# Attention plus MLP layer, one core: where the weight loads are issued, the first projections per token half, and a new written-out order

## The chip, the cores and the metric

The kernel runs on one core of one Trainium2 chip. The metric is device time in microseconds (us). The kernel before takes 318.64 us as the median of five runs (317.17 to 320.43). Its profiled execution took 318.41 us, of which 316.7 us lie between its first and its last instruction (its span).

## The reference, cut to what matters

Sequence 2048, model width 640, 32 heads of 20 columns, MLP width 1728, bf16 in and out.

```
xn = layernorm(x);  q, k, v = xn @ wq, xn @ wk, xn @ wv
for s in range(4):                      # segments of 512 tokens
    p = softmax(q_s k_s^T * scale + causal mask);  a_dot = p v_s
    a_mem = phi(q_s) M / (phi(q_s) z + 1e-6)
    o_s = sigmoid(beta) * a_mem + (1 - sigmoid(beta)) * a_dot
    M += phi(k_s)^T v_s;  z += sum(phi(k_s))      # phi(t) = t+1 if t>0 else exp(t)
h = x + o @ wo
out = h + silu(layernorm(h) @ w1) @ w2
```

## The kernel before, in words

The 2048 tokens are 16 blocks of 128, and four blocks make a segment. For each segment the kernel declares a list of small tasks, each of them a few instructions on one engine. The names below are those of the tasks.

- **Norm.** `n1_st` (statistics, VectorE, L705), `n1_rs` (GpSimd, L714 and L716), `n1_ap` (apply, VectorE, L722), and then a transpose into `xT`. For segment 0 the transpose is a matmul with the identity (`n1_tp`, L731) that ScalarE or VectorE empties (`n1_te`, L740/741); later it is a DMA transpose (`n1_tr`, L746). `n2_*` is the second norm, into `hT`.
- **Weights.** wq and wk arrive raw and are copied into head-padded form in five parts each (`re_wq0` to `re_wk4`, L686/688).
- **Projections.** `pr<s><c><w>` is chunk c of q (w=0) or k (w=1) for the 512 tokens of segment s: five matmuls of 512 columns (L801), emptied by `qe` on ScalarE or VectorE (L811/812). `v<s><i>` is v for one block (L773). `vt<s><n>`, twelve small copies from SBUF to SBUF, collect what is left of the heads into `QKV` (L838); score groups 5 to 7 read it.
- **Attention.** `qk` (scores, L874), `e` (exp on ScalarE, L885), `mk` (causal mask on GpSimd, L897), `av` (L920), `oe`, `tn`, `nm` (VectorE), for eight groups of four heads; segment 0 has them per token half, `x` and `y`. Groups are numbered through: 8s+g.
- **Memory.** `ex` and `ph` build phi, `kt` transposes phi(k) by DMA (L1033), `mz`, `ma` and `mb` update M and z.
- **Back.** `ot` transposes the attention output by DMA (L1094), then `wo` (L1102), the residual `rs` (L1110), the second norm, `h1` (L1126), tanh `th` (ScalarE, L1134), `s` (VectorE, L1140), `h2` (L1157), `o` (L1167), and the store `out` (L1171).

The order of all tasks, and which PSUM bank and which of two engines each uses, is written out by hand in the string `ORDER`; every engine runs its own tasks in the order in which they stand there. A tracker puts in the semaphore waits. `fill54` and its like are matmuls on zeros that keep TensorE running.

All DMAs are issued on SyncE, in one queue. The bulk loads (wo, five parts of w1, five of w2, blocks 8 to 11 of x) carry an `after`: they also wait until a certain attention step of segment 0 has written its output:

```
tick0 = lambda g, h: (f"nm{g}{h}", lambda: [(segs[0]["ot"], [(2 * (h == "y"), g)])])
load_w("wo", ..., after=tick0(0, "x"))
```

Of the kernel before, what the change touches and what calls it, by code (L numbers as in the profile page):

```python
# [5 lines left out]
ACT = mybir.ActivationFunctionType  # L6
# [228 lines left out]
class Graph:  # L235
# [51 lines left out]
    def schedule(self):  # L287
# [3 lines left out]
        for row in ORDER:  # L291
# [14 lines left out]
            t.eng = {"A": AC, "D": DV, "G": PO}[eng] if eng else list(t.engs)[0]  # L306
# [18 lines left out]
D = 640  # L325
# [20 lines left out]
QUAD_SEGS = (0, 1, 2, 3)  # L346

# [8 lines left out]
zpad:0 iota sel epsc x0:0 vpad0 mt2 x2:1 n1_st0:0 x1:2 x3:3 w_q:0 n1_st2:2 mta2 halfc mt0 mt1 n1_rs0 n1_st1:1  # L356
n1_st3:3 epsg0 n1_ap0:0 n1_rs2 fill54:0 n1_tp0:0 n1_te0/A:0 n1_rs1 n1_rs3 n1_ap1:1 n1_ap2:2 n1_tp1:2 n1_te1/A
n1_ap3:0 re_wq0/D:0 n1_tp2:4 n1_te2/D n1_tp3:6 n1_te3/A beta pr000:4 w_k zf0 re_wq1/A pr010:6 lsc0 re_wk0/D:0
re_wk2/A pr001:5 re_wk1/D lsc1 mta1 lsc2 re_wk3/A qe000/D:0 pr011:7 w_wv:0 x4:4,5,6,7 qe001/A qe011/A:0 ex011:0 lsc3
re_wq4/D re_wq2/D pr020:5 qk0x0:0 e0x2:0 e0x0 qe010/D pr031:7 pr021:6 qk1x0:0 vpad1 mtb1 mm5 mm1 mk0x n1_st5:3  # L360
qe020/D:0 ph011:0 qe021/D n1_rs5 v00:4 n1_st6:1 n1_ap5:0 re_wk4/D qe031/A:0 re_wq3/A ex001:1 n1_st4:3 n1_st7:2
e1x2:1 e1x0 v01:6 mk1x pr030:0 ve00/A:0 ex021:0 ve01/A qk2x0:4 qe030/A av1x:1 ex031:2 av0x:2 e2x2:0 pr041:3 pr040:0
oe1x/A:0 e2x0 mt3 n1_rs4 qk3x0:4 e3x0:1 e3x2 n1_rs7 mta3 mtb3 mm11 mk2x n1_rs6 vt06:0 oe0x/D:1 ph001:1 vt09 kt01:0
vt03 tn0x:1 qe041/D:0 kt00:1 ex041:1 v03:2 qe040/D ph031:0 qk0yb0:4 nm0x:0,0 v02:0 e0yb2:0 ve03/D ph021:1 e0yb0
qk0ya0:4 tn1x:2 ve02/D nm1x:0 e0ya2:0 e0ya0 mk0yb mk3x av2x:3 oe2x/D:0 qk4x0:0 av0y:4 e4x2:0 e4x0 n1_ap6:2 av3x:6
mz00:5 tn2x:7 oe0y/D:1 oe3x/D:0 zf1 n1_ap7:1 nm2x:0 qk1yb0:0 vt00 vt010 vt08 vt01 ma00/A:0 e1yb2:0 e1yb0 n1_ap4:3
vt05 n1_tr5:0 mk4x v11:4 ve11/A:1 mk1yb mtb2 mm10 vt07 n1_tr6 vt04 vt011 vt02 mz01:7 qk1ya0:0 tn0y:6 nm0y:0 ma01/D:1
v12:4 ve12/D av4x:7 e1ya2:0 e1ya0 n1_tr4 n1_tr7 oe4x/A:1 tn3x:6 qk5x0:0 e5x0:0 e5x2 mm3 mk5x tn4x:7 nm3x:0 v10:4
qk6x0:0 kt03:0 nm4x:1 e6x0:1 kt02:1 v13:6 e6x2 ve10/D av5x:4 oe5x/D:1 ve13/A qk7x0:0 pr100:5 qe100/D:0 ph041:1
e7x0:0 mz02:4 e7x2 ma02/A:2 mk6x av6x:6 qk2yb0:0 mta0 mk7x e2yb2:1 e2yb0 mk2yb mtb0 tn5x:5 pr101:4 w_w2_1:0 w_w1_0:0  # L370
w_wo:0 oe6x/D:1 av7x:6 nm5x:1 av1y:7 w_w1_3 oe7x/D:0 qk2ya0:0 ex100:1 tn6x:6 qe101/D e2ya2:0 e2ya0 nm6x:1 ex101:0
pr130:5 tn7x:6 pr110:4 nm7x:1 qk3ya0:0 pr111:6 qe110/A:0 ph100:0 ph101:0 pr121:4 oe1y/D:0 ot0:0 qe111/D e3ya2:1
e3ya0 qk3yb0:0 e3yb0:0 wo0:6 qe130/D:0 e3yb2 qe121/D:0 ex110:0 rs0 w_w1_1 ot1 mm0 mzc0 av2y:4 oe2y/A:1 n2_st0:3
qk4ya0:0 mm9 mzc1 mk3yb mm6 mzc6 n2_rs0 mm2 wo1:6 rs1 n2_st1:1 w_w2_0 w_w1_4 n2_ap0:1 e4ya2:0 e4ya0 mz03:4 w_w1_2
qk4yb0:0 kt10:1 e4yb2:1 e4yb0 av3y:5 tn2y:6 pr141:7 n2_rs1 n2_tr0:0 mzc2 mzc3 mb00:0 mk4yb ma03/D:3 nm2y:1 n2_ap1:3
n2_tr1 ex111:1 qk5ya0:0 pr140:4 oe3y/A:1 qe141/A:0 tn3y:7 e5ya0:1 nm3y:1 e5ya2 pr120:6 mz10:7 tn1y:5 qk5yb0:0
qe120/A qe140/D av4y:4 ma10 nm1y:1 oe4y/D:0 ph110:0 e5yb2:0 h1_0_8_0:5 e5yb0 h1_0_1_0:7 th0_8_0:0 ex140:2 th0_1_0:1
tn4y:4 qk6ya0:0 pr131:6 e6ya2:0 e6ya0 s0_1_0:0 nm4y:1 s0_8_0 ph111:0 h1_0_0_0:7 th0_0_0:0 w_w2_2 s0_0_0 qe131/D
mk5yb h1_0_13_0:4 th0_13_0:1 qk6yb0:0 h1_0_10_0:5 h1_0_11_0:7 av5y:6 s0_13_0 e6yb0:1 e6yb2 w_w2_4 x8:8,9,10,11
# [850 lines left out]
```

## Time and profile before

| what | value |
|---|---|
| median of five runs | 318.64 us |
| the profiled execution's own time | 318.41 us |
| its span | 316.7 us |
| TensorE (PE) busy / VectorE (DVE) / ScalarE (ACT) / GpSimd (POOL) | 302.1 / 219.9 / 227.1 / 145.2 us |
| chain that ended last, by engine | PE 73%, ACT 10%, DVE 9%, DMA 3% |
| mean granted TensorE clock | 0.994 |
| weight load wq / wk / wv, issue to landing | 7.1 / 8.7 / 10.4 us |

Busy time of PE is modelled to the end of each matmul, so short groups overlap their own start-up. "Busy" is then no proof that columns stream without gaps. The chain goes back from the last instruction, at each step to what released it. SPq is SyncE's queue of DMA issues, and the idle time in brackets behind an instruction is that of its engine just before it, with what ended it.

### The profile page before, as it was taken

How to read it: one execution, taken by the hardware profiler on the slowest of the kernel's cores; microseconds unless marked ns; L12 is line 12 of the kernel's file. 1: busy time of each engine (PE TensorE's matmuls, PEld its weight loads, DVE VectorE, ACT ScalarE, POOL GpSimd, SP SyncE). 2: the span in 40 equal slices, each digit the busy share in tenths (PEclk: the TensorE clock that was granted, in tenths of full speed). 3: DMA queues.
4: the chain of work that ended last, by engine and by line, in shares of the span. 5: the costliest groups of instructions: out<-in, count | busy, mean ns of one | idle time of the engine just before them, and what ended most of it. 6: DMA issues, size and time to landing. Idle time of an engine off the chain costs nothing.

```text
span 316.7 us, 7256 instructions
## 1 busy us (share of the span) xinstructions
PE 302.1 (95%) x2894; PEld 167.6 (53%) x2894; DVE 219.9 (69%) x488; ACT 227.1 (72%) x322; POOL 145.2 (46%) x282
## 2 busy tenths in 40 slices
PE   8899899999989999999979999999999999999996
PEld 6544444566544555655434544545554457654563
DVE  7778667778878766859987776569866676824703
ACT  1698998899988999889879896778769941004500
POOL 5446652623667565566845345444852831300000
PEclk9999999999999999999979999999999999999999
DMA  6813478967164300032672200041460005330002
GB/s 190 287 23 65 87 213 211 251 175 91 33 122 94 64 2 3 9 70 64 133 117 41 60 2 0 2 92 25 67 83 2 0 2 124 64 106 20 0 2 104
DMA packets 48353, 24.56 MB, mean 78 GB/s; under 512 B 38848, under 2 KB 47232, under 8 KB 48320
## 3 DMA queue, kind: packets, MB, share of 16 engines
q1 hardware_dynamic: 48320, 24.10, 33.9%
q8 instruction: 23, 0.38, 0.5%
q14 instruction: 10, 0.08, 0.1%
HBM read 10.33 MB, written 2.62 MB: 41 GB/s over the span
## 4 chain that ended last, share of the span: by engine, by line
PE 73%; ACT 10%; DVE 9%; DMA 3%; issue 2%; SPq 1%; POOL 1%; DVEq 0%; ACTq 0%
PE ps_all L1157 18%; PE ps_all L1126 18%; PE ps_all L801 10%; PE ps_all L1102 6%; PE ps_all L874 6%; PE ps_all L773 5%; PE ps_all L920 4%; ACT PTE L885 3%; PE ps_all L607 3%; ACT PTB L885 2%; DMA oT<-otok 2%; ACT PTA L885 2%; PE ps_all L949 2%; PE ps_all L953 1%; DMA hT<-xn_rot 1%
## 5 line engine op out<-in xcount | busy, mean ns | idle before, releaser
L1126 PE MATMUL ps_all<-hT,w_sb 128*128 128x512 bf16 (+3 forms) x350 | 69.0, 342 | 1.3 <-DMA hT<-xn_rot 0.8
L885 ACT ACTIVATE PTA<-ps_all 128x1024 bf16<-128x1024 f32 x64 | 62.5, 1028 | 8.4 <-PE ps_all L874 7.5
L1157 PE MATMUL ps_all<-w_sb,sT 128*128 128x320 bf16 x448 | 67.2, 300 | 0.4 <-DVE on L986 0.3
L885 ACT ACTIVATE PTB<-ps_all 128x1024 bf16<-128x1024 f32 (+1 forms) x64 | 59.0, 972 | 8.2 <-PE ps_all L874 8.2
L897 POOL TENSOR_SCALAR_AFFINE_SELECT PTB<-PTB 128x512 bf16<-128x512 bf16 x64 | 40.9, 638 | 43.5 <-ACT PTB L885 41.1
L1134 ACT ACTIVATE th<-ps_all 128x512 f32<-128x512 f32 (+2 forms) x70 | 34.8, 524 | 34.5 <-PE ps_all L1126 30.2
L1140 DVE SCALAR_TENSOR_TENSOR sT<-th,ps_all 128x512 bf16<-128x512 f32 (+2 forms) x70 | 38.9, 576 | 24.1 <-ACT th L1134 23.4
L1157 PEld LDWEIGHTS ps_all<-w_sb,sT 128*128 128x128 bf16 x448 | 40.7, 98 | 24.1 <-issue 7.2
L1126 PEld LDWEIGHTS ps_all<-hT,w_sb 128*128 128x128 bf16 (+1 forms) x350 | 31.8, 99 | 30.6 <-issue 7.2
L885 ACT ACTIVATE PTE<-ps_all 128x1024 bf16<-128x1024 f32 (+1 forms) x40 | 35.9, 946 | 5.1 <-PE ps_all L874 4.7
L897 POOL TENSOR_SCALAR_AFFINE_SELECT PTE<-PTE 128x512 bf16<-128x512 bf16 x40 | 25.7, 641 | 24.3 <-ACT PTE L885 22.9
L705 DVE BATCH_NORM_STATS2 stt<-x_tok 128x6 f32<-128x320 bf16 x64 | 28.0, 479 | 1.9 <-DMA x_tok<-in_A_x_dram 1.5
L1167 DVE SCALAR_TENSOR_TENSOR x_tok<-ps_all,x_tok 128x640 bf16<-128x640 f32 x16 | 13.0, 823 | 19.9 <-PE ps_all L1157 19.7
L1102 PE MATMUL ps_all<-wo_sb,oT 128*128 128x320 bf16 x160 | 24.1, 299 | 2.0 <-DMA oT<-otok 1.1
L801 PE MATMUL ps_all<-xT,wqr 128*128 128x512 bf16 x100 | 24.6, 380 | 0.9 <-ACT xT L740 0.9
L801 PE MATMUL ps_all<-xT,wkr 128*128 128x512 bf16 x100 | 24.4, 380 | 0.0
L773 PE MATMUL ps_all<-wv_sb,xT 128*128 128x320 bf16 x160 | 24.2, 299 | 0.1
L994 POOL TENSOR_TENSOR otok<-on 128x320 bf16<-128x320 bf16 x24 | 19.1, 799 | 11.3 <-DVE on L986 11.3
L812 DVE CAST QK<-ps_all 128x512 bf16<-128x512 f32 x28 | 19.0, 683 | 7.4 <-PE ps_all L801 6.7
L874 PE MATMUL ps_all<-QK 20*128 20x256 bf16 (+3 forms) x360 | 20.8, 288 | 3.0 <-DVE oTs L935 1.8
L897 POOL TENSOR_SCALAR_AFFINE_SELECT PTA<-PTA 128x512 bf16<-128x512 bf16 x24 | 15.4, 641 | 12.3 <-ACT PTA L885 12.3
L935 DVE TENSOR_SCALAR oTs<-ps_all,lsc 128x512 bf16<-128x512 f32 (+1 forms) x25 | 15.6, 628 | 7.3 <-PE ps_all L920 7.0
(78 smaller groups left out, 406.5 us busy)
## 6 DMA issues: line engine op xcount, KB each, us to landing
out_dram<-x_tok SPq DMA_DIRECT2D x16, 160.0 KB, 1.9
w_sb<-in_B_w_dram SPq DMA_DIRECT2D x5, 432.0 KB, 6.0
x_tok<-in_A_x_dram SPq DMA_DIRECT2D x3, 640.0 KB, 6.0
w_sb<-in_B_w_dram SPq DMA_DIRECT2D x3, 640.0 KB, 4.6
QKV<-QK SPq DMA_DIRECT2D x16, 72.0 KB
sT<-in_A_wq_dram SPq DMA_DIRECT2D x1, 800.0 KB, 7.1
sT<-in_A_wk_dram SPq DMA_DIRECT2D x1, 800.0 KB, 8.7
wv_sb<-in_A_wv_dram SPq DMA_DIRECT2D x1, 800.0 KB, 10.4
```

The lines of the kernel that those rows point to most:

```text
L705: T.add(DV, lambda e, hh=hh: e.bn_stats(out=stt[:, s, 6 * hh:6 * hh + 6], in_=xb[:, 320 * hh:320 * hh + 320]), reads=R((xa, xsub)), writes ...
L773: fns.append(lambda e, c=c, hh=hh: e.matmul(bank(ps, hh)[:, 0:320], lhsT=xT[:, c, 128 * i:128 * i + 128], rhs=wv_sb[:, c, 320 * hh:320 * h ...
L801: fns = [lambda e, kc=kc: e.matmul(bank(ps), lhsT=wt[:, kc, c, :], rhs=xT[:, kc, :], start=(kc == 0), stop=(kc == NC - 1)) for kc in range ...
L874: fns.append(lambda e, j=j, o=o, r=r, q0=q0, q1=q1, qa=qa, ka=ka: e.matmul(ps_all[:, o:o + q1 - q0], lhsT=ka[32 * r:32 * r + DH, 128 * j:1 ...
L885: T.add(AC, lambda e: e.activation(out=pt[:, pta.slot, q0:q0 + 2, 0:width], in_=sc3[:, b0:b0 + 2, 0:width], func=ACT.Exp, scale=SCALE), re ...
L897: fns.append(lambda e, v=v: e.affine_select(out=v, in_=v, pattern=[[0, 4], [1, 128]], compare_op=ALU.is_ge, fill=0.0, base=0, channel_mult ...
L994: T.add(PO, lambda e: e.tensor_tensor(out=o_dst, in0=on[:, ona.slot, 0, :].rearrange("p (i x) -> p i x", i=4), in1=on[:, ona.slot, 1, :].r ...
L1102: fns.append(lambda e, c=c, hh=hh: e.matmul(bank(ps, hh)[:, 0:320], lhsT=oT[:, c, 128 * i:128 * i + 128], rhs=wo_sb[:, c, 320 * hh:320 * h ...
L1126: fns = [lambda e, c=c: e.matmul(bank(ps)[0:fw, lo:hi], lhsT=w1_sb[:, c, 128 * f:128 * f + fw], rhs=hT[:, c, lo:hi], start=(c == 0), stop= ...
L1134: T.add(AC, lambda e: e.activation(out=th[0:fw, tha.slot, lo:hi], in_=bank(ps)[0:fw, lo:hi], func=ACT.Tanh, scale=0.5), reads=R((ps, [0])) ...
L1140: T.add(DV, lambda e: e.scalar_tensor_tensor(out=sT[0:fw, f, lo:hi], in0=th[0:fw, tha.slot, lo:hi], scalar=1.0, in1=bank(ps)[0:fw, lo:hi], ...
L1157: fns.append(lambda e, f=f, fw=fw, hh=hh: e.matmul(bank(ps, hh)[:, 0:320], lhsT=sT[0:fw, f, 128 * i:128 * i + 128], rhs=w2_sb[0:fw, f, 320 ...
```

## The change

It has five parts.

1. The loads of wq, wk and wv are issued on ScalarE's DMA queue, ahead of any other work there but a table load and one tiny exp (`warm`). x blocks 0 to 3 and beta stay on SyncE.
2. The bulk loads lose their `after`. In its place they read the region of `re_wk0`'s result, which means that the first of them waits for that copy; from there on only their place in SyncE's queue counts. Blocks 4 to 7 of x (`x4`), which were the ninth issue, without any wait, come under the same rule. `x8` and half of the weights stand right behind it, ahead of the first copy into `QKV`.
3. Chunks 0 and 1 of the projections of segment 0 are made per token half: five matmuls of 256 columns for blocks 0 and 1, and five for blocks 2 and 3. Score tasks of the `x` half wait only for their own half.
4. The parts of h2 are (0,4), (4,7), (7,10), (10,14), w2 is loaded in the same parts, and each part waits for its own piece of w2.
5. `ORDER` is new throughout: 1374 entries in place of 1364. 43 entries name ScalarE and 76 name VectorE, where 45 and 70 did. The zero matmuls are 40, 11, 6 and 3, all near the start; they were 54 at the start, and 2 and 4 just before the first `h1` of segment 1.

The constants with which a planner outside this file weighs tasks (`pe_c`, the `bw` values, `0.4` to `0.46` and the like) change too; no instruction depends on them.

```
-    load_w("q", wraw[:, 0, :, :], cw(A_wq), -96, 2.5, [(sT0, ["q"])])
+    G.task("warm", {AC: 0.3}, lambda e_: T.add(AC, lambda e: e.activation(
+        out=warm[:, :], in_=zpad[:, 0:1], func=ACT.Exp), reads=R((C, ["zpad"])), writes=R((C, ["warm"]))),
+        [(C, ["zpad"])], [(C, ["warm"])], -100)
+    load_w("q", wraw[:, 0, :, :], cw(A_wq), -99, 6.2, [(sT0, ["q"])], "fix", (AC,))
+    load_w("k", wraw[:, 1, :, :], cw(A_wk), -98, 7.8, [(sT0, ["k"])], "fix", (AC,))
+    load_w("wv", wv_sb[:, :, :], cw(A_wv), -97, 9.5, [(W["wv"], [0])], "fix", (AC,))
...
-    load_x(4, 4, -90)
-    load_w("wo", wo_sb[:, :, :], cw(A_wo), 0, 2.5, [(W["wo"], [0])], after=tick0(0, "x"))
...
+        dma("w_" + k, [(W["wk"], [0])] if kind == "plain" else [], wr, lambda e: e.dma_start(out=dst, in_=src), prio, bw, kind, engs=engs)
...
+                for hh, (b0, b1) in enumerate([(0, 2), (2, 4)] if s == 0 and c in SPLIT0 else [(0, 4)]):
...
+                        fns = [lambda e, kc=kc: e.matmul(bank(ps)[:, lo:hi], lhsT=wt[:, kc, c, :], rhs=xT[:, kc, lo:hi],
+                                                         start=(kc == 0), stop=(kc == NC - 1)) for kc in range(NC)]
...
-            parts = ((0, 4), (4, 8), (8, 11), (11, 14))
+            parts = ((0, 4), (4, 7), (7, 10), (10, 14))
+            W2P = ([0], [1], [2], [3, 4])
```

The start of the new order, and its stretch just before the first `h1` of segment 1:

```
zpad:0 warm w_q:0 w_k w_wv:0 mt2 epsc iota vpad1 mt1 vpad0 halfc x0:0 x1:1 x2:2 x3:3 beta sel n1_st0:0 mt0 n1_rs0
n1_st1:2 n1_ap0:0 mt3 fill40:0 n1_tp0:0 mta3 n1_rs1 n1_st3:0 n1_ap1:0 re_wq0/D:0 n1_rs3 fill11:2 n1_tp1:2 n1_ap3:1
n1_st2:2 re_wk1/D:0 n1_te0/A:0 re_wq1/A n1_te1/A fill6:4 n1_tp3:0 n1_te3/A lsc0 pr010x:2 pr000x:3 pr011x:0
...
n2_rs4 n2_st7:0 rs6 wo5:6 mz14:4 qk18a0:0 mb12:0 mb10:0 mk17a n2_ap4:0 n2_rs7 vt27 vt211 vt23 e18a2:0 out2 e18a0
vt26 n2_tr4:0 rs5 n2_ap7:1 n2_tr7 av17:5 h2_3_0:6 qk19b0:0 h2_3_1 n2_st6:2 ma14 e19b0:1 oe17/D:0 tn17:4 h2_3_2 e19b2
qk19a0:0 n2_st5:0 mk18b mk18e n2_rs6 n2_ap6:1 n2_rs5 mk18a mk19b e19a2:1 e19a0 mk19a nm17:1,1 vt25 out0 h2_3_3 vt24
vt28 n2_tr6 mz13:4 n2_ap5:0 o3 ma13 av18:5 n2_tr5 qk20b0:0 tn16:6 av19:4 oe18/D:0 ad17:0 e20b0:0 nm16:1,0 e20b2
oe19/A:1 h1_1_6_0:5 qk21b0:0 th1_6_0:1 s1_6_0:0 tn18:6 e21b2:1 e21b0 nm18:1,1 h1_1_5_0:4 h1_1_1_0:5 th1_5_0:1 out3
```

## The prediction

> **What bounds the kernel now.** I read the page's busy shares first, then a table of busy time by stage, then the chain, then the timeline where the table showed a hole.
>
> ```profile
> PE 302.1 (95%) x2894; PEld 167.6 (53%) x2894; DVE 219.9 (69%) x488; ACT 227.1 (72%) x322; POOL 145.2 (46%) x282
> ```
>
> PE looks full, but it is not streaming all the time. I count the columns of all matmuls from the order, with four row or column tiles side by side counted once, at the rate of the chain's pieces "five matmuls of 512 columns in 1.08 us" (2370 columns per us). They are 266 us, 6.5 of it matmuls on zeros. So some 50 us of 316.7 are waits and group starts. Where they lie is the question.
>
> ```profile
> 12.00:160.00 148.00, 140.78 (x1551) 78.74 (x1549) 112.56 (x276) 133.81 (x199) 84.66 (x166) 1.00 0.45 100
> 170.00:260.00 90.00, 89.38 (x874) 46.50 (x873) 63.16 (x125) 72.39 (x93) 46.14 (x74) 1.00 0.20 33
> 260.00:316.70 56.70, 53.53 (x338) 31.48 (x336) 27.70 (x48) 9.78 (x17) 4.02 (x9) 1.00 0.22 59
> ```
>
> The columns are stretch, PE, PEld, DVE, ACT and POOL busy, clock, DMA share, GB/s. From 170 on PE idles 0.6 us in 90, and then only to the end of the last store; an order gains little there. After the last score group both orders leave the same 60 us of columns. So the change is decided before 170, where ACT (90% busy to 160) and PE wait for each other. PE's real holes to 170, from the timeline: 0.9 at 11.6, 1.4 at 32 to 35, 1.1 at 47 to 57, 1.8 at 89 to 96, 2.05 at 157.5 to 162.6. The last is the largest:
>
> ```profile
> 158.94 3.55 DMA hT<-xn_rot
> 162.57 2.29 PE ps_all L1126 x5
> ```
> ```profile
> 157.50:162.60 5.10, 3.05 (x47) 1.67 (x46) 4.77 (x11) 4.60 (x7) 3.19 (x6) 0.99 1.11 211
> 162.60:167.00 4.40, 4.40 (x20) 1.40 (x21) 3.53 (x9) 2.75 (x5) 1.45 (x4) 0.62 0.26 40
> ```
>
> The chain waits for the last transposed block of the second norm, then five matmuls take 2.29 us instead of 1.08. The clock is 0.62 for 4.4 us, which costs 0.38 x 4.4 = 1.7.
>
> **The stretch before the first h1 of segment 1: 3.5 us gained.** Before, the last `wo` ends at 154.7 and `h1` starts at 162.57: 7.9 us with 3.7 us of useful columns (plus 0.65 of zeros). PE needs 3.7/0.84 = 4.4 for them (0.84: the share at which columns run in the ACT-bound stage, an estimate from 121 us of columns between 11.6 and 162.6, taken without its holes). Lost: 3.5, and 1.7 of clock, 5.2 together. After, 7.9 us of columns stand between the same two points (the last `wo` is wo5), so PE has 9.4 us of work. The chain there is longer: DVE does rs5, ap7, st6, ma14, oe17, st5, ap6, nm17, ap5, by rows 0.8+0.45+1.1+0.3+0.7+1.1+0.45+1.4+0.45 = 6.7, then the transpose 3.55, 10.3 in all. PE waits 0.9, and I give the clock drop 4 chances in 10 (0.7). Gain 5.2 - 1.6 = 3.6, say 3.5; bounds 0 and 5.2.
>
> A rule speaks on the clock. The Trainium skill, "TensorE: Matmul & The Clock Gate", section "What's actually happening", has the slow state after an idle window of about 3.4 us. Here the longest single idle time is 0.77 and the sum 2.05 in 5.1, and the clock fell all the same. By the rule a new order with waits under 3.4 us loses no clock, and the gain here is 4.3; by the row, light work of short groups is enough, and each such stretch may cost 1.7. I follow the row.
>
> **The start: 0.3 us gained (bounds 1.5 each way).** Removed: wq, wk, wv from SyncE's queue, x4's early issue (2.54 us of issuing at 4.76). Added: three issues on ACT (0.43+0.43+0.53) and `warm`; ACT idles 7.6 us there, so they cost nothing; with ACT busy they would cost their 1.4.
>
> ```profile
> 11.59 2.33 PE L801 MATMUL ps_all<-xT,wqr 128*128 128x512 bf16 x10 [0.89 <-ACT xT L740]
> 12.47 0.77 DVE L688 COPY wkr<-sT 128x400 bf16<-128x400 bf16 x4 [1.22 <-DMA sT<-in_A_wk_dram]
> ```
>
> wq lands at 9.8, wk at 12.4. After, GpSimd does a second set of pads (1.9 us) ahead of the first `n1_rs`: it ends at about 6.4 in place of 5.15. The 40 zero matmuls end at 1.12+40x0.152 = 7.2, tp0 at 7.5; eleven (1.7) and tp1 to 9.5; six and tp3 to 10.7. ACT then does re_wq1 (0.85), te1 and te3 (0.65 each), and the first projection starts at about 10.9 if wq lands by 9, 11.3 if at 9.8: 0.3 to 0.7 earlier. The k halves wait for wk plus two copies (0.9). The first exp comes near 16.5 in place of 17.49. But ACT has then done 4 us less of its work, and at score group 4 both orders have as much PE and ACT work behind them; so most of that second is not a gain.
>
> Here a rule speaks against the change: the Trainium skill, "DMA: Bandwidth & Descriptors", section "Issuing engines are not separate DMA queues": a second issuing engine saves only issue time, as all run on the same 16 DMA engines. By it wk lands near 12.2 (beta's 0.52 no longer ahead). The row of 4 to 8 us has DMA share 0.81 and of 0 to 4 0.55: were that filled, 4x0.19 = 0.8 and part of the first stretch are gained, and wk lands near 11. I take 11.5.
>
> Halves: 2x0.65 in place of 1.08 to 1.19 for four projections, 0.5 to 0.9 us of PE; eight evacuations of 256 columns, nearest row 0.48 (128x256 to oTs) against 0.60 to 0.68, 1.4 us in all on ACT and DVE. PE waits for wk in this stretch, which hides it; without that cover it costs 0.9.
>
> **The bulk loads: 0.7 us gained to 60 us (bounds 2.6 gained, 1 lost).** The DMA has room early and none later:
>
> ```profile
> 16.00:20.00 4.00, 4.00 (x33) 1.54 (x32) 2.53 (x7) 3.74 (x7) 0.86 (x2) 1.00 0.01 4
> 52.00:56.00 4.00, 3.56 (x31) 1.68 (x32) 2.44 (x5) 3.54 (x5) 0.34 (x1) 1.00 1.06 189
> ```
>
> The oT transposes at 50 to 57 share with the weights, and half of 1.1 us of holes is what a freer DMA can give back. Now the new wait: x4 waits for `re_wk0`, about 12.9, and behind it in SyncE's queue stand x8, half the weights (2752 KB to the first QKV copy), then 1232 KB among those copies: 4.08 MB. At 327 GB/s (row of 8 to 12) 12.5 us; copies and transposes took 0.41 of 20 to 40, 8.3 us. 12.9+12.5+8.3+2 to land = 35.7, and QKV was first read at 39.39. At 239 GB/s (4 to 8) it is 40.3, 1 us late. So it mostly fits. DVE's st5 waits for x4, at about 14.6 to 16, a stall in which its next evacuation isn't due until 19. h2's own w2 parts cost nothing: all of w2 was there before 77.5, and comes earlier.
>
> **89 to 96: 1.0 us gained of 1.8.** Before, `ot2` stands 0.6 us of columns ahead of `wo2` and `ot3` none ahead of `wo3`, against 2.6 to 3.6 us for the transpose (PE waits 0.69). After they stand 5.4 and 3.4 ahead.
>
> **Elsewhere: 1.5 us lost.** A wholly new order has new meetings of ACT, POOL and PE that no row shows; the holes listed are 7.3 us in 150, and I let it make a fifth of them anew. Bounds 0 and 4. Evacuations move: ACT has some 2 us less in all, DVE 3.5 more; DVE is 76% busy to 160, so nothing on the path.
>
> Sum: -3.5 -0.3 -0.7 -1.0 +1.5 = -4.0. From the profiled execution's 318.4 that is 314.4; the median, 318.64, is 0.2 higher.
>
> **Rivals.** (a) The order only moves its holes: the stretch at 157 keeps half its gain, elsewhere as much is lost: 318.4 -1.8 +1.5 = 318.1. For it: ACT is 90% busy to 160 and its work hardly shrinks. Chance 0.15. (b) All holes close, with ACT at 95%: 318.4 - 7.3 - 1.7 = 309.4. For it: those waits are short and of many kinds, so an order can meet them. Against: DVE is later than before at `ap5`. 0.13. (c) Slower, by the unpaced x loads: DVE takes its tasks in order, and st5 and st11 wait for x4 and x8. A 640 KB load of x took 2.3 to 11.5 us. If x4 lands later than 17 (4 us after issue) and x8 after 21, DVE empties no PSUM, PE stops up to 5 us and the clock falls (1.7): 314.4 +6.7 +0.5 = 321.6. It decides from a landing of 6 us on. Against: the 11.5 was behind 2.4 MB in the same queue, here only wv's rest. 0.12. The forecast has 0.60.
>
> **Numbers.** A measurement tells from no change only more than about 0.5%, 1.6 us. Faster by more: forecast, (b), together 0.73; within: (a) less its edges, 0.14; slower: (c) and a little of (a), 0.13. The range takes the forecast's bounds, (a) and most of (b): 309.2 to 319.3.
>
> **What would show it.** The stretch before the first h1 of segment 1: PE idle under 1 us and no row of clock below 0.9. First exp on PTE at 16 to 17. wk's landing 11 to 12. QKV copies landed before the first score of group 5. No DVE wait for x_tok above 2 us. PE columns from 170 on as before. Wrong if x4 or x8 hold DVE, if the clock falls in the first 20 us, or if ACT's idle time to 160 isn't smaller than 14.2.

## The result and the profile after

| | before | after |
|---|---|---|
| median | 319.02 us (45 runs) | 316.58 us (24 runs) |
| lowest to highest | 317.17 to 322.06 | 314.98 to 318.11 |
| profiled execution, own time | 318.41 us | 315.29 us |
| its span, its mean clock | 316.7 us, 0.994 | 313.6 us, 1.000 |

The ratio is 0.992, with a 95% interval of 0.9902 to 0.9939. So the change gains 2.4 us, where 4.0 was forecast; the two profiled executions differ by 3.1.

The executions of both kernels fall into two groups by their mean granted clock, and this bears on everything below. Ratios and counts here use the executions within 1.5% of the fastest of their kernel, which are 48 of the 52 of before that ran beside after and beside the experiments. Of these 48, 23 had a clock of 0.998 or more, with a median of 317.65 us, and 25 a lower one, with 319.66. Of 25 executions of after, 12 were at 0.998 or more (315.28) and 13 lower (316.94). The profile of before is one of the lower kind, that of after one of the higher.

The first line of the profile after, engine busy times and instructions:

```profile
PE 301.9 (96%) x2914; PEld 168.9 (54%) x2914; DVE 224.8 (72%) x491; ACT 225.6 (72%) x324; POOL 144.7 (46%) x282
```

Busy time of PE is 0.2 us less than before, and the span is 3.1 us less: what was won is waiting time. Busy time by stretch, after (stretch, PE, PEld, DVE, ACT, POOL, clock, DMA share, GB/s):

```profile
160.00:165.00 5.00, 5.00 (x39) 2.13 (x38) 3.08 (x7) 4.99 (x8) 1.76 (x3) 1.00 0.45 131
...
12.00:160.00 148.00, 142.49 (x1589) 80.14 (x1587) 118.64 (x283) 134.52 (x202) 82.08 (x162) 1.00 0.43 96
...
80.00:90.00 10.00, 9.80 (x104) 5.85 (x103) 6.34 (x15) 9.97 (x16) 6.16 (x11) 1.00 0.44 85
90.00:100.00 10.00, 9.94 (x98) 5.33 (x97) 8.19 (x20) 9.28 (x12) 5.39 (x11) 1.00 0.63 102
```

The same two stretches of before:

```profile
80.00:90.00 10.00, 9.30 (x97) 5.42 (x95) 8.16 (x22) 9.38 (x13) 6.30 (x14) 1.00 0.30 51
90.00:100.00 10.00, 8.83 (x94) 4.70 (x93) 7.97 (x19) 8.73 (x11) 7.35 (x14) 1.00 0.55 113
```

From 12 to 160 us PE is busy 1.7 us more, and 1.6 of that lies between 80 and 100: the hole of 89 to 96 is gone. In the row of 160 to 165 the clock is 1.00, where before has 0.75, with the 0.62 of 162.6 to 167 in it. The chain there, after (start, us, what):

```profile
155.94 3.39 DMA hT<-xn_rot
...
159.38 1.25 PE ps_all L1131 x5
```

The last transposed block of the second norm still ends the chain, and takes as long as before (3.39 us against 3.55). But PE had other work for all but 0.20 us of it, and the five matmuls of `h1` take 1.25 in place of 2.29. That stretch went as forecast. The start did not. DMA issues of the first 20 us, after (kind, issuing queue, number, KB each, median us from issue to landing):

```profile
sT<-in_A_wq_dram ACTq DMA_DIRECT2D x1, 800.0 KB, 5.3
...
x_tok<-in_A_x_dram SPq DMA_DIRECT2D x4, 160.0 KB, 5.1
```

Before, from the same view:

```profile
x_tok<-in_A_x_dram SPq DMA_DIRECT2D x4, 160.0 KB, 3.1
```

The row of 4 to 8 us, in which these loads share the DMA engines, first after, then before. The last number, what they moved, is 378 GB/s in place of 239:

```profile
4.00:8.00 4.00, 4.00 (x28) 3.10 (x27) 1.66 (x6) 0.00 (x0) 2.04 (x7) 1.00 1.06 378
```
```profile
4.00:8.00 4.00, 4.00 (x32) 3.27 (x31) 3.39 (x11) 0.00 (x0) 2.39 (x8) 1.00 0.81 239
```

And the timeline after, where these loads are waited for (start, busy us, engine, what, idle time before it and what ended it):

```profile
8.97 0.89 DVE L704 BATCH_NORM_STATS2 stt<-x_tok 128x6 f32<-128x320 bf16 x2 [2.28 <-DMA x_tok<-in_A_x_dram]
...
12.04 1.15 PE L806 MATMUL ps_all<-xT,wqr 128*128 128x256 bf16 x9
```

wq, issued at 1.1, lands at 6.4 in place of 9.75, but the small x blocks take 5.1 us in place of 3.1. VectorE waits 2.28 us for block 3, and the first projection starts at 12.04, 0.45 later than before. Two further waits stand out. The first, 1.15 us, is longer than the one that before has at that place (0.91 us, at 32.67). It lies in the stretch in which the bulk loads, the copies into `QKV` and the `xT` transposes share SyncE's queue, and behind it, at 35.16, PE waits another 0.37 for the transposed block 5. The second, at an output projection near the end, is new:

```profile
33.49 0.40 PE L878 MATMUL ps_all<-QK 20*128 20x256 bf16 x8 [1.15 <-DVE otok L972]
```
```profile
263.99 1.26 PE L1107 MATMUL ps_all<-wo_sb,oT 128*128 128x320 bf16 x8 [0.73 <-DMA oT<-otok]
```

To see where the two kernels part, I read off when each trace has the same number of matmul columns behind it. Columns are counted in us at the prediction's rate, and matmuls on zeros are left out, as the two kernels have them in different places; 259.9 us remain in either. At 5 to 15 us of columns, after is 0.7 to 1.0 us behind before; at 30 to 65 it is 2.0 to 2.9 behind, at 70 to 120 0.6 to 1.6. At 125 it is 3.6 ahead, from there on 2.9 to 4.1, and it ends 3.1 ahead. So the first 65 us lose, and the gain comes in two places: some 2.0 us at the hole of 89 to 96 (from 65 to 70 us of columns), and 4.7 in the stretch before the first `h1` of segment 1 (from 120 to 125).

### The profile page after: what moved, and what is told of

It is laid out like the page before. It is cut to its first block, busy times and chain, and to the rows that moved or that the text cites. A ratio compares the mean times of both kernels' runs of the same rounds, so it can differ in the third digit from the quotient of the medians.

```text
span 313.6 us, 7306 instructions
## 1 busy us (share of the span) xinstructions
PE 301.9 (96%) x2914; PEld 168.9 (54%) x2914; DVE 224.8 (72%) x491; ACT 225.6 (72%) x324; POOL 144.7 (46%) x282
## 4 chain that ended last, share of the span: by engine, by line
PE 70%; ACT 13%; DMA 7%; DVE 5%; issue 2%; SPq 2%; POOL 1%; ACTq 0%; DVEq 0%
PE ps_all L1163 18%; PE ps_all L1131 15%; PE ps_all L806 11%; PE ps_all L878 7%; PE ps_all L1107 6%; PE ps_all L772 5%; ACT PTA L889 4%; PE ps_all L924 4%; ACT PTB L889 4%; ACT PTE L889 3%; DMA x_tok<-in_A_x_dram 2%; DMA QKV<-QK 1%; DVE sT L1145 1%; DMA oT<-otok 1%; PE ps_all L957 1%
## 5 line engine op out<-in xcount | busy, mean ns | idle before, releaser
L1131 PE MATMUL ps_all<-hT,w_sb 128*128 128x512 bf16 (+3 forms) x350 | 67.5, 337 | 0.4 <-DMA hT<-xn_rot 0.2
L1163 PE MATMUL ps_all<-w_sb,sT 128*128 128x320 bf16 (+1 forms) x448 | 67.7, 300 | 0.0
L1139 ACT ACTIVATE th<-ps_all 128x512 f32<-128x512 f32 (+3 forms) x70 | 35.1, 519 | 35.3 <-PE ps_all L1131 30.2
L1145 DVE SCALAR_TENSOR_TENSOR sT<-th,ps_all 128x512 bf16<-128x512 f32 (+3 forms) x70 | 39.0, 574 | 26.4 <-ACT th L1139 25.8
L1163 PEld LDWEIGHTS ps_all<-w_sb,sT 128*128 128x128 bf16 (+1 forms) x448 | 40.7, 98 | 22.5 <-issue 7.9
L901 POOL TENSOR_SCALAR_AFFINE_SELECT PTE<-PTE 128x512 bf16<-128x512 bf16 x40 | 25.5, 638 | 30.3 <-ACT PTE L889 28.9
L806 PE MATMUL ps_all<-xT,wqr 128*128 128x512 bf16 (+1 forms) x110 | 24.8, 361 | 0.4 <-ACT QK L814 0.4
L806 PE MATMUL ps_all<-xT,wkr 128*128 128x512 bf16 (+1 forms) x110 | 25.0, 361 | 0.0
L815 DVE CAST QK<-ps_all 128x512 bf16<-128x512 f32 (+1 forms) x31 | 20.1, 655 | 6.0 <-PE ps_all L806 5.7
L713 POOL TENSOR_TENSOR rst<-mvt,eps_c 128x1 f32<-128x1 f32 x32 | 6.7, 209 | 30.9 <-DVE mvt L707 30.9
L990 DVE TENSOR_TENSOR on<-ps_all,rd 128x640 bf16<-128x640 f32 x24 | 19.8, 824 | 0.8
```

Of the source, the lines that this page charges most:

```text
L806: fns = [lambda e, kc=kc: e.matmul(bank(ps)[:, lo:hi], lhsT=wt[:, kc, c, :], rhs=xT[:, kc, lo:hi], start=(kc == 0), stop=(kc == NC - 1)) f ...
L815: (lambda e: e.tensor_copy(out=o, in_=i_))
L901: fns.append(lambda e, v=v: e.affine_select(out=v, in_=v, pattern=[[0, 4], [1, 128]], compare_op=ALU.is_ge, fill=0.0, base=0, channel_mult ...
L1131: fns = [lambda e, c=c: e.matmul(bank(ps)[0:fw, lo:hi], lhsT=w1_sb[:, c, 128 * f:128 * f + fw], rhs=hT[:, c, lo:hi], start=(c == 0), stop= ...
L1139: T.add(AC, lambda e: e.activation(out=th[0:fw, tha.slot, lo:hi], in_=bank(ps)[0:fw, lo:hi], func=ACT.Tanh, scale=0.5), reads=R((ps, [0])) ...
L1145: T.add(DV, lambda e: e.scalar_tensor_tensor(out=sT[0:fw, f, lo:hi], in0=th[0:fw, tha.slot, lo:hi], scalar=1.0, in1=bank(ps)[0:fw, lo:hi], ...
```

## The experiments

The theory was that of the prediction, now with its places: the new order wins in those two stretches; the second queue and the unpaced loads by themselves win nothing. The rivals were that the holes only move, that early loads or early weights are the gain, and that later stages take up what the start loses. Each run's ratio is to before on the same chip; against after, medians are compared.

**1. The stretch put back into after.** In `ORDER`:

```
-... rs6 wo5:6 mz14:4 ... rs5 n2_ap7:1 n2_tr7 av17:5 h2_3_0:6 qk19b0:0 h2_3_1 ... h2_3_2 ... h2_3_3 ... o3
+... rs6 h2_3_0:6 h2_3_1 h2_3_2 h2_3_3 o3 mz14:4 ... n2_ap7:1 n2_tr7 av17:5 wo5:6 rs5 qk19b0:0 ...
```

> The kernel after, with only the stretch before the first h1 of segment 1 put back to the arrangement of before: h2_3_0 to h2_3_3 and o3 run ahead of the last output projection (wo5), whose residual and second norm then have little behind them to cover them. Theory: PE waits 1.5 to 2.5 us for the transposed hT, the clock falls to about 0.6 for some 4 us, and 2.5 to 4.5 us of the gain go, so that it stands at 319 to 321, at or above before. Rival (the stretch is not where the gain is; PE has slack later that takes it up): under 1 us slower than after.

Measured: 322.69 us, ratio 1.0108 (1.0064 to 1.0151), 6.1 above after. The stretch by stages:

```profile
155.00:160.00 5.00, 1.74 (x23) 0.60 (x20) 4.53 (x12) 2.74 (x4) 1.34 (x4) 0.86 0.45 101
160.00:165.00 5.00, 3.95 (x44) 1.78 (x48) 3.04 (x7) 2.32 (x4) 3.39 (x6) 0.50 0.68 103
```

PE is busy 5.7 us of 10 and the clock falls to 0.50. Up to 115 us of columns the trace is within 1.1 us of after; at 125 it is 6.3 behind, and it stays 6.1 to 6.5 behind to the end. So the stretch is where the gain is. The loss is above the forecast's 2.5 to 4.5, and much of it is clock: at 0.86 and 0.50 the two rows lose 3.2 us. All six executions of this kernel had a mean clock of 0.989 or less, so here the fall came every time. That the wait itself is long because VectorE, which has nine tenths of its time filled from 155 to 160, gets its work for the last block only after the last output projection is my reading of the order; no run tests it. The same trace, whose order up to 146 us is that of after, shows something else:

```profile
32.00:34.00 2.00, 0.58 (x16) 0.12 (x8) 1.97 (x6) 2.00 (x5) 1.32 (x3) 1.00 0.78 107
...
36.00:38.00 2.00, 2.00 (x15) 0.81 (x14) 1.80 (x4) 0.47 (x1) 1.03 (x2) 0.50 0.52 98
```

After the wait of 32 to 34 us the clock is 0.94, 0.50 and 0.71 in the next three rows of two microseconds: 1.7 us of clock, as much as at 162 in the profile of before. In the profiled execution of after the same wait left the clock at 1.00.

**2. The stretch repaired in before, first try.** `wo6` is taken up ahead of the four parts of `h2_3`, which go down behind it:

```
-... wo4:2 ... h2_3_0:0 qk18b0:4 tn16:2 h2_3_1 h2_3_2 ... h2_3_3 ... wo7:2 ... wo6:0 ... av17:2
+... wo4:2 ... wo6:0 qk18b0:4 tn16:2 ... wo7:2 ... h2_3_0:0 ... av17:2 h2_3_1 ... h2_3_2 h2_3_3
```

> The kernel before, with nothing of the change but a repaired stretch before the first h1 of segment 1: the last output projection (wo6) goes up ahead of h2_3_0 to h2_3_3, and the four parts of h2_3 go down behind it as cover for its residual, second norm and transpose. Theory (most of the gain is this stretch: waits 1.8 plus the clock drop 1.7): 3 to 3.5 us faster than before, PE idle ahead of the first h1 of segment 1 under 0.6, five h1 matmuls in 1.1 to 1.3 us, no row of clock 0.62 there. Rival (the waits only move on, ACT is the bound to 170 us): within 1 us of before. Rival (the gain of the new order lies in the hole of 89 to 96 and many small ones): 1 to 1.7 us faster, the clock alone.

Measured: 329.16 us, ratio 1.0271 (1.0216 to 1.0325). Neither the theory nor a rival held, and the chain says why:

```profile
150.20 0.58 SPq L1169
...
150.84 3.88 DMA oT<-otok
...
154.76 2.85 PE ps_all L1100 x10
```

L1169 is the line of the stores, and `ot7` is issued behind one. The parts of `h2_3` had been what PE did until `ot7` landed; without them `wo7` waits, and its ten matmuls take 2.85 us instead of 1.53, at a clock of 0.50 from 155 to 160. Nor is the wait before `h1` gone: the last transposed block lands at 173.36, after 4.40 us, and `h1` starts at 173.45. Besides what is shown, the edit moves some small tasks of the same stretch (x12, o3, out3 and parts of the second norm of block 6).

**3. The stretch repaired in before, second try.** Only `wo6` and its residual, statistics, `n2_rs` and apply go up; `h2_3` stays ahead of `wo7`:

```
-... h2_3_0:0 qk18b0:4 tn16:2 h2_3_1 h2_3_2 nm16:0,1 ... wo7:2 ... rs7 n2_st7:1 ... wo6:0 ... mk18a rs6 n2_st6:3 n2_rs7 ...
+... h2_3_0:0 qk18b0:4 wo6:2 h2_3_1 h2_3_2 rs6 n2_st6:0 tn16:2 nm16:0,1 ... wo7:2 ... rs7 n2_st7:1 n2_rs7 ... mk18a ...
```

> The kernel before, with the stretch before the first h1 of segment 1 repaired in another way than by taking the parts of h2_3 out (that left wo7 waiting for its transposed oT): only wo6 goes up, five microseconds, behind h2_3_0, with its residual, statistics and apply; h2_3 stays ahead of wo7. Theory (the stretch itself is worth its waits and its clock): the first h1 of segment 1 starts 1.5 to 3.5 us earlier than 162.57, no row of clock 0.62 there, and the time is 1.5 to 3.5 us below before. Rival (VectorE is the bound there, 94% busy from 157.5 to 162.6, so moving matmuls only moves the wait): within 1 us of before.

Measured: 323.7 us, ratio 1.0149 (1.0104 to 1.0193), and `h1` starts at 169.65. The timeline:

```profile
159.26 0.19 POOL L712 TENSOR_TENSOR rst<-mvt,eps_c 128x1 f32<-128x1 f32 x1 [2.93 <-DVE mvt L706]
...
162.09 0.64 POOL L895 TENSOR_SCALAR_AFFINE_SELECT PTA<-PTA 128x512 bf16<-128x512 bf16 x1
...
162.78 0.62 PE L918 MATMUL ps_all<-PTA,Vx 128*32 128x512 bf16 x4 [2.77 <-POOL PTA L895]
```

My edit had put `n2_rs7` ahead of the causal mask `mk18a` on GpSimd. GpSimd then stood 2.93 us waiting for VectorE's statistics, the mask behind it came late, and `av18` waited 2.77 us for the mask; after that the clock was 0.66 from 160 to 170. In the profiles of both tries, moreover, the clock fell at 34 to 38 us as in experiment 1, in a part that is not edited, which is 1.3 us of either sum. (This edit also takes the apply of block 7 and the transposes of blocks 6 and 7 up.) So the two tries do not show what the stretch alone would be worth in before. They show that an order is not repaired by moving one engine's task: what came with PE's move, a task of two short instructions on GpSimd, made the wait.

**4. wq, wk, wv back on SyncE.**

```
-    load_w("q", ..., "fix", (AC,))      # and k, wv
+    load_w("q", ..., "fix", (SP,))      # ORDER: x3:3 w_q:0 w_k w_wv:0 beta
```

> The kernel after, with wq, wk and wv issued on SyncE behind the four single x blocks, as before; ScalarE keeps only its table load and the tiny exp. Theory (the second queue brings wq early but slows the x blocks, so it gains nothing): x3 lands at about 6 in place of 8.97, wq near 10, first projection at 11.3 to 12.1, time within 0.6 us of after either way. Rival (the second queue is worth its 0.3 to 1 us): 0.5 to 1.5 us slower than after. Rival (the second queue costs): 0.5 to 1 us faster.

Measured: 315.29 us, ratio 0.988 (0.9844 to 0.9916), 1.3 below after. The first projection starts at 10.97 instead of 12.04. But then:

```profile
13.90 0.23 ACT L614 ACTIVATE bsel<-beta_bc 128x32 f32<-128x32 bf16 x1 [2.06 <-DMA beta_bc<-in_A_beta_dram]
...
14.85 0.34 PE L876 MATMUL ps_all<-QK 20*128 20x256 bf16 x8 [1.38 <-ACT QK L812]
```

beta, now last in the queue, lands at 13.88, ScalarE waits for it in `lsc0`, and the copies for the first scores stand behind. So most of the 1.07 was lost again at once, and the trace ends 0.5 ahead of after. The other 0.8 of the medians may lie in the clock: 5 of 6 executions were at 0.998 or more, against 12 of 25 of after. At such clocks alone the medians are 314.88 and after's 315.28, and the intervals overlap, so it is not shown that this version is faster than after.

**5. The second queue alone, in before.**

```
-    load_w("q", wraw[:, 0, :, :], cw(A_wq), -96, 2.5, [(sT0, ["q"])])
+    load_w("q", wraw[:, 0, :, :], cw(A_wq), -96, 2.5, [(sT0, ["q"])], engs=(AC,))   # and k, wv; ORDER: zpad:0 w_q:0 w_k w_wv:0 ...
```

> The kernel before, with the first part of the change alone: wq, wk and wv are issued first, on ScalarE's DMA queue, and the x blocks stay on SyncE. Projections are still made for all 512 tokens at once. Theory (a second queue brings wq 3 us earlier at the cost of the x blocks, which then land at 5 to 9 us in place of 3.5 to 5.7, and only the halves make that bearable): the first projection starts at 12.5 to 14 in place of 11.59, and the time is 1 to 2.5 us above before. Rival (earlier weights help in any case): the first projection starts at 10.5 to 11.3, and the time is 0.3 to 1.5 us below before.

Measured: 323.29 us as the median of all executions, which reach from 318.67 to 326.51; the ratio, to which 7 of the 14 count, is 1.006 (1.0017 to 1.0103), 1.9 us. From the view of the DMA issues:

```profile
x_tok<-in_A_x_dram SPq DMA_DIRECT2D x4, 160.0 KB, 5.7
```

wq takes 5.3 us, and the x blocks 5.7 instead of 3.1; they land at 3.9, 6.6, 7.8 and 8.8 (before 3.1, 3.5, 5.7 and 6.1). The first projection starts at 13.14, 1.55 later. By the ratio the forecast of this experiment held (by the medians of all executions the loss is 4.0, more than forecast); its rival, a gain, is out. (The clock fell in this trace too: 0.50 in the row of 36 to 38 and 0.53 in that of 165 to 170.) From 4 to 8 us the DMA moved 376 GB/s instead of 239, so idle time was filled, and x4, issued early here as in before, was in at 14.2 instead of 16.3. But the last weight landed at 14.9 instead of 14.6: for the weights as a whole nothing was won, and what the second queue changed is mainly who comes first, wq and not x.

**6. The halves undone, in after.**

```
-SPLIT0 = (0, 1)                         # n1_te3 lsc0 pr010x pr000x ... n1_rs2 n1_ap2 n1_tp2 n1_te2
+SPLIT0 = ()                             # n1_te3 n1_rs2 n1_ap2 n1_tp2 n1_te2 lsc0 pr010 pr000 ...
```

> The kernel after, with the third part undone: chunks 0 and 1 of the first projections are made for all 512 tokens at once, behind the transposes of all four blocks, so that the third transpose stands ahead of them. Theory (the halves cost 0.5 to 0.9 us of TensorE behind cover and let ScalarE begin earlier): the first exp starts 1 to 2 us later than 17.07, and the time is 0.3 to 1.5 us above after. Rival (the early start of ScalarE isn't worth anything, the halves only cost): 0.3 to 0.9 us below after.

Measured: 323.1 us, ratio 1.0127 (1.0079 to 1.0176), 6.5 above after, far outside both. The chain of the start (start, us, what):

```profile
2.21 7.04 DMA x_tok<-in_A_x_dram
...
9.28 0.90 DVE stt L702 x2
...
14.57 0.73 PE ps_all L728 x5
...
16.08 6.77 PE ps_all L804 x20
```

The row of 16 to 18 us (clock, DMA share and GB/s stand last):

```profile
16.00:18.00 2.00, 1.92 (x5) 0.74 (x6) 0.00 (x0) 0.14 (x2) 0.51 (x2) 0.50 0.87 241
```

x3 lands at 9.25; VectorE takes block 3 ahead of block 2, so all four projections wait until 16.08, and their matmuls then take 6.77 us where four such groups in before took 4.5 (from 11.59 to 16.08). PE waits 2.06 us ahead of 14.57 and 0.80 ahead of 16.08, and the clock is 0.50 from 14 to 20 us and 0.83 in the next row: 3.4 us, about half of the loss, are clock. So with the order of after, the halves are what lets the late x blocks do little harm. How much they are worth with x on time was not tried: the order of blocks 2 and 3 on VectorE is made for the halves.

**7. Six bulk loads later, in after.**

```
-... x8/S:8,9,10,11 ... w_w2_4/S:0 w_w2_1/S ... w_w2_2/S w_w1_3/S:0 vt09:0 vt00 vt03 w_wo/S:0 w_w1_2/S vt06 ... kt01:0
+... x8/S:8,9,10,11 ... vt09:0 vt00 vt03 vt06 ... w_wo/S:0 w_w1_3/S:0 w_w1_2/S w_w2_4/S:0 w_w2_1/S w_w2_2/S kt01:0
```

> The kernel after, with six of the bulk loads (wo, two parts of w1, three of w2; 2112 KB of the 2752 KB) taken from ahead of and between the first copies into QKV and put behind them, just ahead of the first DMA transpose of phi(k). Theory (early bulk loads delay the QKV copies and the xT transposes of blocks 4 to 7, which is what after loses between columns 30 and 50): the score of group 5 starts 1 to 1.5 us earlier than 41.13, the holes of 33 to 36 shrink, and the oT transposes of 50 to 60 are slower; in all 0.5 faster to 1 slower than after. Rival (early loading is the gain): 1 to 2.5 us slower. Rival (early loading costs): 1 to 2 us faster.

Measured: 323.86 us, ratio 1.0148 (1.0107 to 1.0188), 7.3 above after.

```profile
43.43 0.52 SPq L563
...
45.91 6.80 DMA phiKt<-phiK
```

The six loads are 2704 KB. The first transpose of phi(k) behind them, issued at 43.99, takes 8.2 us from issue to landing, where it takes 2.4 in after; the second, the line above, takes 6.80 in place of 3.9. PE waits 6.6 us for it, and the clock behind that wait is 0.66 from 50 to 60. In this run and the next, what counts is not early or late but what stands right behind the loads.

**8. The early loads alone, in before.**

```
-    load_w("wo", ..., after=tick0(0, "x"))          # and w1, w2, x8
+    load_w("wo", ..., )                             # reads W["wk"], declared behind the copies of wk
-... vt06:0 ... vt03 ... w_w2_1:0 w_w1_0:0 w_wo:0 ... w_w1_3 ...
+... x8:8,9,10,11 w_w2_4:0 w_w2_1 w_w2_2 w_w1_3:0 vt06:0 ... vt03 w_wo:0 w_w1_2 ...
```

> The kernel before, with the second part of the change alone: the bulk loads lose their waits for attention steps and read the first part of the padded wk instead; x8, wo, two parts of w1 and three of w2 are issued from the end of the x4 and wv loads on, ahead of and among the first copies into QKV; x4 keeps its early issue. Theory by the predicted sum: 0 to 1.5 us faster than before, from the oT transposes of 50 to 57. Rival (early loads delay QKV copies and xT transposes by as much as they free later): within 0.5 of before. Rival (they cost): 0.5 to 1.5 us slower.

Measured: 323.91 us, ratio 1.0159 (1.0102 to 1.0215).

```profile
27.20 5.72 DMA phiKt<-phiK
...
32.95 0.67 DVE phiK L820
...
34.37 0.73 DVE Vx L780
```

It is the same mechanism by a longer way. wo and a part of w1 stand just ahead of a transpose of phi(k). The next phi(k) uses the same buffer, so VectorE waits for the transpose until 32.92, and takes its other tasks only behind it: PE waits 3.1 us at 33 for an evacuation, and the clock behind it is 0.72, 0.50 and 0.92 in the rows from 36 to 42. The theory of the prediction (0 to 1.5 us gained) fell. In after the transposes of phi(k) stand behind the copies, with no load ahead of them; that is what the new order does for the unpaced loads.

The same trace has a second thing to show. Its order before the first `h1` of segment 1 is that of before, and the wait there is longer than in the profile of before:

```profile
165.00:170.00 5.00, 3.15 (x36) 1.31 (x37) 4.46 (x13) 3.39 (x6) 2.85 (x6) 1.00 0.67 73
```
```profile
167.97 1.24 PE L1122 MATMUL ps_all<-hT,w_sb 128*128 128x512 bf16 x5 [1.27 <-DMA hT<-xn_rot]
```

PE waits 1.27 us (0.77 in the profile of before), and yet the clock stays at 1.00 and the five matmuls take 1.24 us instead of 2.29. So the fall that the prediction read there is not paid by every execution of that order.

**9 to 12. Versions of after without its remaining waits.** All have wq, wk and wv on SyncE, except the third.

```
9:  beta w_q w_k w_wv behind x3; w_wo, w_w1_2 behind kt02; nm1x ahead of ve03; n1_tr5 ahead of vt05, vt02
10: as 9, but w_q beta w_k w_wv; re_wq0 behind n1_ap3; re_wq1 behind n1_te1; lsc0, zf0 behind qe001x; oe3x ahead of ve03
11: after itself, with fill6:2 ahead of qk0ya0
12: as 10, but nm1x, oe3x and ve03 as in after; fill6:2 ahead of qk0ya0; h2_11_2 ahead of wo15
```

> The kernel after with four edits: beta, wq, wk, wv issued on SyncE behind the x blocks in this order (beta first, so that ScalarE's two exps of beta don't hold the copies for the first scores, as they did until 13.9 with beta last); wo and one part of w1 issued behind the second transpose of phi(k), in a stretch in which the queues are empty; the normalization of group 1 ahead of VectorE's copy of v03; the transpose of block 5 ahead of two copies into QKV. Theory (the start and the hole of 32 to 36 us are what after still loses): first scores at 13.5 in place of 14.85, the hole of 32 to 36 at 1 us or less and without a fall of the clock in any run, time 312.5 to 314.5. Rival (ScalarE is the bound to 150 us, and what is won early is waited for later): 314.8 to 315.8, as with the weights on SyncE alone.

Measured: 315.01 us, ratio 0.9882 (0.9835 to 0.993). First scores at 14.73 and not at 13.5: with beta ahead of it wq lands at 10.79, and VectorE, in whose order wq's copies stand ahead of the apply of block 3, waits. The transpose of block 5 lands at 33.57 instead of 35.12 and its wait is gone, but the one ahead of it is 1.30. At equal columns this trace goes from 0.4 behind after at 5 to 15 us to 0.5 ahead at 30 to 70, so it takes back 0.9 of what after loses there. The forecast was too low by 0.5; the range of the rival holds it.

> The kernel after, as in the last version with weights on SyncE, but with wq ahead of beta, the two copies of wq behind the apply of block 3 and the emptying of the second transpose, ScalarE's two exps of beta behind the first four evacuations, and the evacuation of group 3's output ahead of the copy of v03. Theory (time lost in the first 40 us stays lost, as no later stretch takes it up): first projection at 10.3 to 11, first scores near 13.5 in place of 14.73, the wait at 32.7 under 0.6; 312.8 to 314.2 in all. Rival (ScalarE, 90% busy later, takes up what is won early): 314.7 to 315.5, no better than the last version.

Measured: 314.66 us, ratio 0.9872 (0.9828 to 0.9917), between the two forecasts and nearer to the rival's. First projection at 10.84, first scores at 14.25, and the wait at 33 is still 1.3 us. The chain around it:

```profile
30.34 1.51 ACT PTB L887 x2
31.85 0.70 ACT ex L819 x2
...
32.77 1.52 ACT PTE L887 x2
```

The wait now ends with the copy of v03 on VectorE, but the chain runs through ScalarE, without a gap worth the name from 30.34 to 34.29: so for this place the rival, ScalarE as the bound, fits. But little was brought to it: of the start's 1.2 us at the first projection 0.09 is left at the first scores (14.25 against after's 14.34) and at the first exp (16.98 against 17.07), as the k halves wait for wk, which lands at 12.48. So the run shows ScalarE's chain, and cannot tell what would have become of a larger lead.

> The kernel after, with six matmuls on zeros added in the wait at 32.3 to 33.5 us, ahead of the scores that wait for VectorE. Theory (the clock falls in that hole in about half of all runs of the kernel after, and this makes its two groups of times, near 315.3 and near 317): all or nearly all runs have a mean clock of 0.998 or more, median 315.0 to 315.6. Rival (the clock falls elsewhere or for another reason): clocks of 0.994 in a third or more of the runs, median 316 to 317. The zeros themselves may cost up to 0.3.

Measured: 315.47 us, ratio 0.9883 (0.9839 to 0.9927), and all 6 executions at a clock of 0.999 or more. In its trace:

```profile
32.00:34.00 2.00, 1.69 (x32) 0.84 (x30) 1.97 (x5) 2.00 (x4) 1.73 (x4) 1.00 0.85 127
...
36.00:38.00 2.00, 2.00 (x22) 1.20 (x21) 1.97 (x4) 0.89 (x2) 1.37 (x3) 1.00 0.52 98
```

This is what the theory of the clock expects. If every execution had after's chance (13 of 25) of a lower clock, six without one would come about once in 80 times. It is no clean test, though: after itself has three of its zero matmuls at 34.3 us, in that same wait, where the text on the change puts them all near the start (57 of the 60 are done by 11.3 us).

> The kernel after with what the runs so far point to, taken together: wq, beta, wk, wv on SyncE behind the x blocks; ScalarE's two exps of beta and two copies of wq later, as in the last version; six zero matmuls in the wait at 32.5 us (VectorE's order there as in after); the transpose of block 5 ahead of two copies into QKV, and wo and one part of w1 behind the second transpose of phi(k); a part of h2 ahead of the output projection that waits 0.73 for its transpose at 263 us. Theory (start, clock and that wait add up, since nothing later takes them up): clock 0.998 or more in all runs, 313.3 to 314.6. Rival (what is won up to 40 us is waited for again): 314.8 to 315.6, the same as the versions with one of these edits.

Measured: 313.4 us, ratio 0.9883 (0.9817 to 0.9949). Four of six executions took 313.08 to 313.45 at a clock of 0.999 or more, where after's at such clocks took 314.98 to 316.62; so the edits do add up to about 2 us there. The other two took 316.63 and 317.42 at 0.995, in spite of the same zeros. Where the clock fell in those two was not profiled. The versions 4, 9 and 10, without the six zeros, had 5, 4 and 5 of 6 at a high clock, the versions 11 and 12, with them, 6 and 4. So it is shown that the clock falls in the wait of 33 us in some executions, and not shown that six zero matmuls prevent it. Version 12 has the lowest median of all; it was not run beside after on one chip, and its interval overlaps after's.

## Why the prediction was right and where it was wrong

**The total** came out at 316.6 instead of 314.4, on the right side and within the range. There is luck in that: two parts were off by 3.9 us one way, three by 3.0 together the other way, and these errors in part cancelled.

**The stretch before the first h1 of segment 1** (3.5 gained) was right in mechanism and nearly in size. PE waits 0.20 where I allowed 0.9. At equal columns after goes from 1.1 behind to 3.6 ahead, 4.7 us between the two profiled executions, of which up to 1.7 is the clock in that of before. The other 3.0 stand against the 3.5 - 0.9 = 2.6 that I had without the clock. Putting the old arrangement back costs 6.1, about half of it clock.

**The clock inside it** was the term that I misjudged. I read 1.7 us from one trace in which the clock fell, and took it as a cost that every execution of before pays and 4 in 10 of after. In fact 25 of 48 executions of before have a lower clock, and 13 of 25 of after, and experiment 8 has a longer wait at that place without a fall. Nor did the chance of a fall go down: in experiment 1, whose order is after's up to there, the clock falls at 34 to 40 us. It did so at 34 to 38 in the traces of experiments 2, 3 and 5 as well, which have before's order there. Where it fell in the other executions of before and after was not profiled. Taken at high clocks alone the change gains 317.65 - 315.28 = 2.4, at low clocks 2.7. A profile at 0.994 against one at 1.000 shows 3.1, so up to 0.7 of that is the choice of executions.

The rule that I weighed, an idle window of about 3.4 us in the Trainium skill, "TensorE: Matmul & The Clock Gate", section "What's actually happening", does not tell these cases apart: at 33 us PE waited 1.14 us in the execution of experiment 1 in which the clock fell, and 1.15 in the profiled one of after, in which it did not. No wait there comes near 3.4. My row was right in that waits of about 1 us can be enough, and misread in that they do it every time. What decides is open.

**The start** (0.3 gained) had the wrong sign: 0.45 lost at the first projection, 0.7 to 1.0 at 5 to 15 us of columns. I costed the landing of wq and wk and left out what their queue does to the x blocks, which I took from before as they stood. GpSimd's second set of pads, which I let hold the first `n1_rs` to 6.4 us, did not: it ended at 5.2. wk landed at 11.0, nearer to what I let the idle DMA rows say (11.5, or 11 if filled) than to the rule's 12.2 (which my own terms, 12.4 less beta's 0.52, would have put at 11.9); the row of 4 to 8 did fill, with 378 GB/s in place of 239. But the weights together gained little. With one queue (experiment 4) wq, wk and wv land at 9.4, 11.6 and 13.7, with two at 6.4, 11.0 and 13.0, and x pays for it with 2 us. That is how far the rule of "DMA: Bandwidth & Descriptors", section "Issuing engines are not separate DMA queues", that a second issuing engine saves only issue time, bears here: the last weight comes 0.7 us earlier. wq is also issued earlier in after (at 1.1 us, in before at 2.7), and no run separates that from the second queue.

**"Most of that second is not a gain"**, as ScalarE has as much work behind it, is half answered. What is lost stays lost: in experiments 1, 4 and 7 a delay is the same to 0.1 us over 35 us of columns and more, so no later stage takes it up in that stretch. Whether what is won early waits for ScalarE was not tested, as experiment 10 brought only 0.09 us to the first exp; that ScalarE's chain runs without a gap from 30.3 to 34.3 speaks for it.

**The bulk loads** (0.7 gained to 60 us) had the wrong sign as well, as far as the loss is theirs: between 15 and 65 us of columns, after falls from 0.7 to 2.9 behind. QKV's copies landed in time for segment 0, as forecast. What I had not seen is the issue time of SyncE's queue. The source of the transpose of block 5 was ready at about 30.0; the transpose was issued at 31.78, behind nine copies of 0.64 to 0.89 us each and two loads, and landed at 35.12. How the 2.2 us divide between loads, copies and the order of VectorE is not shown; experiment 9, which changes a little of each, takes 0.9 back. Experiments 7 and 8 show the larger danger, a transpose right behind a load.

**89 to 96** (1.0 gained) was too small: PE is busy 1.6 us more from 80 to 100, and at equal columns 2.0 us come back between 65 and 70.

**Elsewhere** (1.5 lost) came out at some 0.7, which is about the wait of 0.73 at 263.

So in the profiled pair start and bulk loads lose 2.9 where 1.0 was to be gained, 3.9 worse than forecast. The hole of 89 to 96 is 1.0 better, the stretch 1.2 and elsewhere 0.8: 3.1 in place of 4.0. The medians give 0.7 less, by the clock of the two profiled executions.

The rivals: (a) described the first 65 us well and nothing behind it; (b) did not happen; (c) had the right mechanism, VectorE behind a load of x, at x3 instead of x4, and with 2.28 us instead of 5. VectorE did wait 2.93 us for x4 as well, which landed at 17.8, past my point of decision; PE had matmuls to do meanwhile. Of the signs that I named, no clock below 0.9, PE idle under 1 us, QKV in time and less idle time of ScalarE from 12 to 160 (13.5 us against 14.2) came true. The first exp at 17.07 just missed its 16 to 17, "no wait for x above 2 us" did not hold, and "from 170 on as before" only to 263. One sign of being wrong came true: x4 held VectorE.

## What to carry to other kernels

Before a load goes to a second queue, ask whose bytes it overtakes: a large load won 3.4 us and small ones lost 2, which did little harm only because the first consumer was split so as not to need the late ones. Behind a bulk load never put a transfer that an in-order engine waits for through a buffer; and when moving a task, go through every engine on which it issues something, since a tiny wait on GpSimd or SyncE holds everything behind it. When one trace shows a fall of the clock, look at the clock of many executions before counting it as a cost that a change can remove.

## What the runs showed of the hardware that was not expected

- Loads of 800 KB on a second queue, issued together with four loads of 160 KB on the first, made their median landing 5.1 to 5.7 us instead of 3.1.
- A DMA transpose took 2.3 to 4.4 us from issue to landing behind other transposes and copies, and 5.6 to 8.2 us behind bulk loads in the same queue (experiments 7 and 8, and before at 56.2 and 69.0 us).
- The granted clock fell to 0.50 to 0.71 for about 4 us behind waits of TensorE of which the longest were 0.77 to 1.14 us (before at 162 us, experiment 1 at 34). A wait of 1.15 us in the profile of after, and one of 1.27 in that of experiment 8, left it at 1.00. About half of the executions of one and the same program have a lower mean clock, and they take 1.7 to 2.0 us more.
